# Two attention blocks mixed by a gate: the two products with K of a group in block B stand on either side of the two products for the row maxima

## The chip, the cores and the metric

The kernel runs on one NeuronCore of a Trainium2 chip. The metric is the device time of one execution in microseconds (us). A difference under 0.3% of it cannot be told from none.

## The reference, cut to what matters

Two attention blocks read the same `x` (2048 x 512, 32 heads of 16) and are mixed by a gate for each row. Block A is an attention in four segments of 512 rows with a causal mask inside each, plus a memory `M`, `z` that is carried from segment to segment; block B is a full softmax attention over all 2048 rows.

```python
# A, for each of N = 4 segments
logits = jnp.einsum("bhqd,bhkd->bhqk", qs, ks) * scale + mask
a_dot  = jnp.einsum("bhqk,bhkd->bhqd", _softmax(logits, axis=-1), vs)
o      = g * a_mem + (1.0 - g) * a_dot
...
# B
scores = jnp.einsum("bhqd,bhkd->bhqk", q, k) * (Dh ** -0.5)
o      = jnp.einsum("bhqk,bhkd->bhqd", _softmax(scores, axis=-1), v)
...
return g * a + (1 - g) * b
```

## The kernel before

Up to about 335 us of the profiled execution the kernel projects `x` to Q, K and V and runs A's memory. Then comes the main loop over `k` (L932), 32 **units**. Unit `k` treats four heads of one 512-row chunk of queries, once for block B (`ub = 32 + k`) and once for block A (`ua = k`). It runs over `n`: `n` 0 to 31 are the **groups** of B, 32 to 36 the groups of A. All is written out in program order; each engine works through its own queue in that order and waits at semaphores.

A group of B (`t_group`, L516) treats 128 keys and two of the four heads:

- Two **products with K** (L528), transposed scores, keys on the partitions and 512 queries in the free dimension. The first has its operands on partitions 0 to 63, the second on 64 to 127, so the two stand in two halves of TensorE's rows. Below they are **T0** and **T1**. Each goes to a PSUM bank of its own.
- The banks come from `T3 = TB + [MB]` (`tb0`, `tb1`, `mb`; L848). `bank()` gives out the one that was given out longest ago (L88). So with three banks T0 of a group takes the bank that T1 of the group before the last one had, and T1 takes the bank of T0 of the group just before.
- Two exponentials on ScalarE (L534), **exp0** for T0 and **exp1** for T1, from the bank to the tile `raw8`. A bank is free for the next product when its exponential is done.

Behind the group come the tasks that `plan` holds for `(k, n)`. In B's groups that is, up to unit 30, group 19, one call of `s_b` (L467), in the first groups of unit 0 two: the **products for the maxima** of the *next* unit (128 queries on the partitions, 512 keys in the free dimension), **S1** on rows 64 to 127 first, then **S0** on rows 0 to 63, into the two halves of one of the two buffers `sbk0`, `sbk1`, and one maximum over both on VectorE (L476, **the reduce**). S1 must wait until the reduce of two calls before has left its buffer. `s_a` (L442) does the same for A, in A's groups.

Then `pvs` (L853) issues the **products with V** (L550, all 128 rows) for the tile of keys before, with the exponentials as operand; in the groups `n` = 0 it issues A's last ones and `fin_copy` (L553), a copy of the sums by VectorE. In the group `n` = 1 there are none; from unit 9 on `out_mm` (L612), 12 products of the output projection, stands there.

Other work of VectorE that is queued between the reduces of B's groups: `fin_rec` behind the groups 11 and 13 (L571, two small operations each), `m_chain` behind the group 21 (L480, four), and in every other unit an addition of `out_mm`. Behind the group 24 `m_rows` (L497) issues two products (L501) into a bank of `T3` and a copy on ScalarE.

Of the kernel before, what the change touches and what calls it, by code (L numbers as in the profile page):

```python
# [23 lines left out]
NT = SEQ // 128  # L24
# [10 lines left out]
def gated_mix_kernel(ctx, tc, xt, wq, wk, wv, wo, beta, wqkv, wob, gate_w, out):  # L35
# [52 lines left out]
    def bank(allowed):  # L88
        b = min(allowed, key=lambda a: max([n for n, x in enumerate(lru) if x is a], default=-1))
        lru[:] = [x for x in lru if x is not b] + [b]  # L90
        return b
# [308 lines left out]
    def q_of(u):  # L400
        return QA[u % 2] if u < 32 else QB[u % 3]

    def k_of(u, p):
        return KA[u % 2][:, p] if u < 32 else KB[(u - 32) % 3][:, p]

    def load_q(u):
        kd, qd, c = UN[u]
        load_qk(q_of(u), kd, 0, qd, c)

    def load_ka(u):  # L410
        kd, qd, c = UN[u]
        load_qk(KA[u % 2], kd, 1, qd, c)

    def load_kb(k, c=None):
        dst = KB[k % 3] if c is None else KB[k % 3][:, :, c * C:(c + 1) * C]
        load_qk(dst, "B", 1, k % 8, c)
# [6 lines left out]
    def load_vb(g):  # L423
        v_src(VB[g % 2], "B", g % 4, None)

    def load_va(u):
        kd, qd, c = UN[u]
        v_src(VA[(u // 2) % 2], "A", qd // 2, c)
# [51 lines left out]
    def m_chain(k):  # L480
        mx = pair_max(k)
        if k == 1:
            nc.vector.memset(mx[:, 0], 0.0)
        if k < 32:
            nc.vector.tensor_reduce(mx[:, 1], MXB.pop(32 + k).rearrange("q j p i c -> q (j p) i c"), axis=AX.X,
                                    op=OP.max)
        else:
            nc.vector.memset(mx[:, 1], 0.0)
        del MX[k]
        mx = mx.rearrange("q u h i -> q (u h i)")  # L490
        m8 = M8[k] = W.tile([128, 2, 32], FT, name="m8")
        hi = W.tile([128, 32], FR, name="mhi")
        nc.vector.tensor_scalar(hi, mx, -1.0, None, op0=OP.mult)
        nc.vector.tensor_copy(m8[:, 0], hi)
        nc.vector.scalar_tensor_tensor(m8[:, 1], mx, -1.0, hi, op0=OP.mult, op1=OP.subtract)
# [17 lines left out]

    GA = (((0, (0, 1)),), ((0, (2, 3)),), ((1, (0, 1)), (3, (0, 1))), ((1, (2, 3)), (3, (2, 3))), ((2, (0, 1)), (2, (2, 3))))

    def t_group(u, n, banks):  # L516


        kd, qd, c = UN[u]
        bs = [bank(banks) for _ in range(2)]  # L520
        c0 = 0
        for it, hs in (((n // 2, (n % 2 * 2, n % 2 * 2 + 1)),) if kd == "B" else GA[n]):
            q0 = 128 * it if kd == "A" else 0
            w = C - q0
            pn = it if kd == "B" else it % 2
            for j, h in enumerate(hs):
                r = slice(64 * j, 64 * j + 64)
                nc.tensor.matmul(bs[j][:, c0:c0 + w], k_of(u, h // 2)[r, 128 * it:128 * it + 128],  # L528
                                 q_of(u)[r, h // 2, q0:], start=True, stop=True)
                PT[u, it, h] = PTILE[pn % 2][:, 2 + j if (kd, it) == ("A", 2) else h][:, c0:c0 + w]  # L530
            c0 += w
        for j in range(2):
            pt = PTILE[pn % 2][:, 2 + j if (kd, n) == ("A", 4) else hs[j]]
            nc.scalar.activation(pt, bs[j], AF.Exp, scale=SCALE)  # L534
            if kd == "A":
                m = pt[:, :128] if n < 2 else pt.rearrange("p (a t) -> p a t", a=4)[:, ::3 if n < 4 else 2]
                nc.gpsimd.affine_select(out=m, in_=m, pattern=[[1, 128]] if n < 2 else [[0, 2], [1, 128]],  # L537
                                        compare_op=OP.is_ge, fill=0.0, base=0, channel_multiplier=-1)
# [59 lines left out]
    def load_wo(g):  # L598
        for a, w in enumerate((wo, wob)):
            raw = AT["o"][1][:, g, a]  # L600
            nc.sync.dma_start(raw, w[g * 128:(g + 1) * 128, :])
            nc.gpsimd.tensor_copy(AT["wh"][:, g, a], raw)
            nc.gpsimd.tensor_tensor(AT["wl"][:, g, a], raw, AT["wh"][:, g, a], op=OP.subtract)
# [146 lines left out]
    for blk in range(16):  # L750
# [9 lines left out]
        n = blk + 1 + (c == 2)  # L760
# [74 lines left out]
    def late():  # L835
        proj.close()
        L = AT["L"] = ctx.enter_context(tc.tile_pool(name="late", bufs=1))
        VB[1] = L.tile([128, NT, 8, E + 1], FT, name="vb1")
        AT["o"] = [L.tile([128, 4, 2, C], FT, name=f"o{n}") for n in range(2)]
        AT["wh"] = L.tile([128, 4, 2, DM], FR, name="wh")  # L840
        AT["wl"] = L.tile([128, 4, 2, DM], FR, name="wl")
        AT["d"] = [L.tile([128, C], FT, name=f"d{n}") for n in range(2)]
        AT["oh"] = L.tile([128, 4, 2, 128], FR, name="oh")
        AT["ol"] = L.tile([128, 4, 2, 128], FR, name="ol")
        for p in range(2):
            set_aux(KB[2][:, p], 0)
# [6 lines left out]
    def pvs(k, n):  # L853

        ua, ub = k, 32 + k
        if n == 0:
            if k:
                pv(ua - 1, 2)
                fin_copy(ua - 1)
        elif k == 31 and n < 2 * NT:  # L860
            if n % 2 and n > 1:
                pv(ub, n // 2 - 1)
        elif 2 <= n < 2 * NT + 2:
            pv(ub, n // 2 - 1, n % 2 * 256, n % 2 * 256 + 256)
            if n == 2 * NT + 1:
                fin_copy(ub)
        elif n > 2 * NT + 1:
            m = n - 2 * NT - 2
            if m < 2:
                pv(ua, 0, 256 * m, 256 * m + 256)  # L870
            else:
                pv(ua, 1)
                pv(ua, 3)
# [13 lines left out]
    def beside(k, it):  # L887

        for f, it0, u in ((fin_load, NT + 1, 32 + k), (fin_rec, 5, 31 + k), (fin_bc, 6, 31 + k),
                          (fin_load, 1, k - 1), (fin_rec, 6, k - 1), (fin_bc, S_LAST + 2, k - 1)):  # L890
            if it == it0 and (k or it0 > NT):
                f(u)
        c, j = divmod(k - 1, 8)
        if k and j % 2:
            for kd, it0 in (("B", 9), ("A", 13)):
                if it == it0:
                    fin_norm(kd, j // 2, c)
        if k >= 8 and k % 2 == 0 and it == NT + 2:
            out_split(k // 8 - 1, k // 2 % 4)
        if (k, it) == (31, 4):  # L900
            grest = AT["grest"] = AT["o"][0][64:, 0, 0]
            nc.sync.dma_start(grest, GD[3 * C:].rearrange("(o t) -> o t", o=1).to_broadcast([64, C]))
        if (k, it) == (31, 9):
            grest = AT["grest"]
            nc.vector.tensor_scalar(grest, grest, nh[64:, 3:4], None, op0=OP.mult)
        if (k, it) == (31, NT + 2):
            fin_rec(63)
        if k == 31 and it == 13:
            o = AT["o"][1][:64, 3, 0]
            nc.gpsimd.tensor_tensor(o, o, AT["d"][0][:64], op=OP.mult)  # L910
        if k == 31 and it < 8 and it % 2 == 0:
            for a in range(2):
                tail_split(it // 2, slice(0, 3), a)
# [3 lines left out]
    plan = {}  # L917
# [14 lines left out]
    for k in range(32):  # L932
        ua, ub = k, 32 + k
        banks = T3 + [b[:, 0] for b in SBK] * (k == 31)
        for n in range(NG):
            it = n // 2 if n < NG - 1 else NT + 2
            t_group(*(ub, n) if n < 2 * NT else (ua, n - 2 * NT), banks)
            for f in plan.get((k, n), []) + ex[k][0].get(n, []):
                f()
            pvs(k, n)  # L940
            for f in ex[k][1].get(n, []):
                f()
            if n % 2 == 0 and n < NG - 1:
                continue
            beside(k, it)
            if it == S_LAST:
                m_chain(k + 1)
            if it == 4 and not k:
                late()
            if it == 4 and not k:  # L950
                load_q(ub + 2)
                for c in range(NC4):
                    load_kb(2, c)
            if it == NT and k < 29:
                load_q(ub + 3)
                load_kb(k + 3)
            if it == 6 and k < 31:
                load_q(ua + 1)
                load_ka(ua + 1)
                if (ua + 1) % 2 == 0:  # L960
                    load_va(ua + 1)
            if it == 9:
                if k % 2 == 0 and k < 30:
                    load_vb(k // 2 + 1)
                if 1 <= k <= 4:
                    load_wo(k - 1)
# [55 lines left out]
```

## Time and profile before

| | us |
|---|---|
| median of 3 runs | 1959.55 |
| lowest and highest | 1957.34, 1963.12 |
| profiled execution | 1956.4 |
| its span | 1954.7 |
| busy PE (matmul) in the span | 1930.3 |
| busy DVE (VectorE) | 1629.9 |
| busy ACT (ScalarE) | 1433.4 |
| busy POOL (GpSimd) | 275.8 |

The profile comes from one execution. In a row of the view in order of time stand the start (us from the span's start), the duration (us; of a merged row, from the first start to the last end), the engine, the line of the kernel, the operation, what it writes and reads with buffer numbers left out, and the count; in brackets the idle time ahead of it and what ended that. PE is the matmul itself, PEld the load of its stationary operand. In the trace the reduce is `mxb<-sbk`, an exponential `raw<-tb` or `raw<-mb`, a product with K `tb<-` or `mb<-`, one for the maxima `sbk<-`, one with V `pvb<-`. K of block B lies in `kb` or `xh`, so `tb<-qb,kb` and `tb<-qb,xh` are the same kind of product.

In the view of waits a row has engine, tile, line, what ended the wait, total us, number of waits and the longest.

### The profile page before, as it was taken

How to read it: one execution, taken by the hardware profiler on the slowest of the kernel's cores; microseconds unless marked ns; L12 is line 12 of the kernel's file. 1: busy time of each engine (PE TensorE's matmuls, PEld its weight loads, DVE VectorE, ACT ScalarE, POOL GpSimd, SP SyncE). 2: the span in 40 equal slices, each digit the busy share in tenths (PEclk: the TensorE clock that was granted, in tenths of full speed). 3: DMA queues.
4: the chain of work that ended last, by engine and by line, in shares of the span. 5: the costliest groups of instructions: out<-in, count | busy, mean ns of one | idle time of the engine just before them, and what ended most of it. 6: DMA issues, size and time to landing. Idle time of an engine off the chain costs nothing.

```text
span 1954.7 us, 43539 instructions
## 1 busy us (share of the span) xinstructions
PE 1930.3 (99%) x17485; PEld 939.3 (48%) x17485; DVE 1629.9 (83%) x1798; ACT 1433.4 (73%) x2699; POOL 275.8 (14%) x497
## 2 busy tenths in 40 slices
PE   7999999999999999999999999999999999999999
PEld 5887777444344444444444444444444444444445
DVE  7135766899999999999999999999999999999942
ACT  4233333688888888888888888888888888888884
POOL 5201000012120101111111111111111111111022
PEclk9999999999999999999999999999999999999999
DMA  7666655644444444343435453444354444434111
GB/s 218 170 205 188 198 192 178 156 98 115 98 115 93 106 91 109 81 111 80 114 87 115 87 115 87 113 87 115 87 115 87 109 86 96 101 88 106 48 50 58
DMA packets 163790, 222.49 MB, mean 114 GB/s; under 512 B 39916, under 2 KB 90556, under 8 KB 157828
## 3 DMA queue, kind: packets, MB, share of 16 engines
q1 hardware_dynamic: 159284, 211.41, 43.7%
q0 software_dynamic: 3248, 8.03, 2.1%
q8 instruction: 138, 2.26, 0.5%
q14 instruction: 64, 0.52, 0.1%
q10 hardware_dynamic: 1056, 0.26, 0.1%
HBM read 147.95 MB, written 68.16 MB: 111 GB/s over the span
## 4 chain that ended last, share of the span: by engine, by line
PE 95%; DVE 3%; ACT 1%; SPq 1%; DMA 1%; issue 0%; DVEq 0%; ACTq 0%
PE pvb L550 33%; PE tb L528 17%; PE sbk L474 12%; PE mb L528 9%; PE tb L304 4%; PE sbk L452 3%; PE tb L616 2%; PE mb L304 2%; PE sbk L287 1%; DVE mxb L476 1%; PE tb L287 1%; PE pvb L304 1%; PE mb L616 1%; PE sbk L456 1%; PE mb L287 1%; PE pvb L287 1%
## 5 line engine op out<-in xcount | busy, mean ns | idle before, releaser
L476 DVE TENSOR_REDUCE mxb<-sbk 128x2 f32<-128x1024 f32 x1024 | 1222.3, 1222 | 67.3 <-PE sbk L474 63.1
L534 ACT ACTIVATE raw<-tb 128x512 f32<-128x512 f32 x1555 | 887.5, 598 | 152.9 <-PE tb L528 89.6
L550 PE MATMUL pvb<-raw,vb 128*17 128x256 f32 (+1 forms) x8072 | 639.3, 388 | 0.0
L534 ACT ACTIVATE raw<-mb 128x512 f32<-128x512 f32 x782 | 467.6, 598 | 79.5 <-PE tb L528 44.8
L528 PE MATMUL tb<-qb,xh 64*128 64x512 f32 x872 | 331.6, 495 | 1.7 <-ACT raw L534 1.7
L550 PEld LDWEIGHTS pvb<-raw,vb 128*17 128x17 f32 x8072 | 134.4, 95 | 340.1 <-issue 336.6
L474 PE MATMUL sbk<-xh,qb 64*128 64x512 f32 x1344 | 281.5, 395 | 2.7 <-DVE mxb L476 1.8
L528 PE MATMUL mb<-qb,xh 64*128 64x512 f32 x445 | 220.6, 496 | 0.0
L537 POOL TENSOR_SCALAR_AFFINE_SELECT raw<-raw 128x256 f32<-128x256 f32 (+1 forms) x320 | 115.5, 361 | 709.6 <-ACT raw L534 701.7
L528 PEld LDWEIGHTS tb<-qb,xh 64*128 64x128 f32 x872 | 124.7, 183 | 179.6 <-issue 89.9
L528 PE MATMUL tb<-qb,kb 64*128 64x512 f32 x470 | 179.5, 496 | 1.3 <-DVE st L314 0.8
L460 DVE TENSOR_REDUCE mx<-sbk 128x2 f32<-128x768 f32 (+1 forms) x128 | 136.7, 1090 | 22.9 <-PE sbk L456 18.3
L474 PE MATMUL sbk<-kb,qb 64*128 64x512 f32 x704 | 146.4, 398 | 0.0
L474 PEld LDWEIGHTS sbk<-xh,qb 64*128 64x128 f32 x1344 | 138.3, 186 | 7.4 <-DVE mxb L476 5.0
L528 PEld LDWEIGHTS mb<-qb,xh 64*128 64x128 f32 x445 | 81.3, 183 | 95.2 <-issue 50.4
L590 POOL TENSOR_TENSOR o<-o,d 128x512 f32<-128x512 f32 x31 | 39.7, 1281 | 545.6 <-DMA d<-rd 461.9
L528 PEld LDWEIGHTS tb<-qb,kb 64*128 64x128 f32 x470 | 68.2, 183 | 100.1 <-issue 52.6
L528 PE MATMUL mb<-qb,kb 64*128 64x512 f32 x234 | 116.1, 496 | 0.0
L550 PE MATMUL pvb<-raw,va 128*17 128x256 f32 (+2 forms) x1280 | 94.7, 384 | 0.8 <-ACT pvs L559 0.8
L452 PE MATMUL sbk<-ka,qa 64*128 64x256 f32 (+3 forms) x512 | 88.2, 358 | 1.1
L528 PE MATMUL tb<-qa,ka 64*128 64x512 f32 (+3 forms) x339 | 79.5, 372 | 0.0
L311 ACT ACTIVATE st<-tb 128x512 fp32r<-128x512 f32 x33 | 19.8, 599 | 80.2 <-DVE phi L310 40.5
(284 smaller groups left out, 1837.6 us busy)
## 6 DMA issues: line engine op xcount, KB each, us to landing
xh<-dB SPq DMA_DIRECT2D x38, 512.0 KB
vb<-vdB SPq DMA_DIRECT2D x16, 1088.0 KB
dB<-st SPq DMA_DIRECT2D x64, 256.0 KB
dA<-st SPq DMA_DIRECT2D x64, 256.0 KB
pd<-pvs SPq DMA_DIRECT2D x64, 256.0 KB
kb<-dB SPq DMA_DIRECT2D x22, 512.0 KB
xh<-dB SPq DMA_DIRECT2D x38, 256.0 KB
qb<-dB SPq DMA_DIRECT2D x64, 128.0 KB
```

Source lines behind the costliest of these rows:

```text
L287: nc.tensor.matmul(b, lhs, WV[wi][:, k, :], start=n == 0, stop=n == 11)
L304: nc.tensor.matmul(b, WS[ws][w][wi][:, k, :], (XH, XL)[xi][c][:, k, :], start=n == 0, stop=n == 11)
L452: nc.tensor.matmul(b[:, j, c0:c0 + n], q_of(u)[r, p, i * 128:(i + 1) * 128], k_of(u, p)[r, :n], start=True, stop=False)
L460: nc.vector.tensor_reduce(m[:, :, p, i], b[:, :, :n], axis=AX.X, op=OP.max)
L474: nc.tensor.matmul(b[:, j], q_of(u)[r, p, i * 128:(i + 1) * 128], k_of(u, p)[r, kc * C:(kc + 1) * C], start=True, stop=True)
L476: nc.vector.tensor_reduce(MXB[u][:, :, p, i, kc], b, axis=AX.X, op=OP.max)
L528: nc.tensor.matmul(bs[j][:, c0:c0 + w], k_of(u, h // 2)[r, 128 * it:128 * it + 128], q_of(u)[r, h // 2, q0:], start=True, stop=True)
L534: nc.scalar.activation(pt, bs[j], AF.Exp, scale=SCALE)
L537: nc.gpsimd.affine_select(out=m, in_=m, pattern=[[1, 128]] if n < 2 else [[0, 2], [1, 128]], compare_op=OP.is_ge, fill=0.0, base=0, channe ...
L550: nc.tensor.matmul(PVB[32 * h:32 * h + E + 1, q0 + lo:q0 + hi], vt[:, it, 4 * q + h, :], pt[:, lo:hi], start=it == 0 and lo == 0, stop=it ...
L590: nc.gpsimd.tensor_tensor(o, o, d, op=OP.mult)
L616: nc.tensor.matmul(b, (AT["oh"], AT["ol"])[oi][:, g, a], (AT["wh"], AT["wl"])[wi][:, g, a], start=n == 0, stop=n == 11)
```

## The change

`t_group` takes a list `between` and calls it ahead of the second of the two products. In the main loop the plan's tasks of a group of B are taken out of the plan and given to `t_group` so. The order T0, T1, S1, S0 becomes T0, S1, S0, T1. A's groups and B's groups without a task stay.

```diff
-    def t_group(u, n, banks):
+    def t_group(u, n, banks, between=()):
...
             for j, h in enumerate(hs):
+                if j:
+                    for f in between:
+                        f()
                 r = slice(64 * j, 64 * j + 64)
                 nc.tensor.matmul(bs[j][:, c0:c0 + w], k_of(u, h // 2)[r, 128 * it:128 * it + 128],
                                  q_of(u)[r, h // 2, q0:], start=True, stop=True)
...
-            t_group(*(ub, n) if n < 2 * NT else (ua, n - 2 * NT), banks)
+            mid = plan.pop((k, n)) if n < 2 * NT and (k, n) in plan else []
+            t_group(*(ub, n) if n < 2 * NT else (ua, n - 2 * NT), banks, mid)
             for f in plan.get((k, n), []) + ex[k][0].get(n, []):
                 f()
```

The queue of TensorE, two groups in the middle of unit 9, before (`tb_110`, `tb_111` and `mb` are the three banks, `sbk_115` and `sbk_114` the buffers of the maxima; what a row waits for stands in brackets):

```order
L528 MATMUL tb_111<-qb_70,kb_89 128x512
L528 MATMUL tb_110<-qb_70,kb_89 128x512 [waits Activation_49]
L474 MATMUL sbk_115<-xh_88,qb_69 128x512 [waits DVE_49]
L474 MATMUL sbk_115<-xh_88,qb_69 128x512
L550 MATMUL pvb<-raw_86,vb_75 17x256 x4
L528 MATMUL mb<-qb_70,kb_89 128x512 [waits Activation_49]
L528 MATMUL tb_111<-qb_70,kb_89 128x512 [waits Activation_49]
L474 MATMUL sbk_114<-xh_88,qb_69 128x512 [waits DVE_49]
L474 MATMUL sbk_114<-xh_88,qb_69 128x512
```

And the same groups on the same engine after the change:

```order
L531 MATMUL tb_111<-qb_70,kb_89 128x512
L474 MATMUL sbk_115<-xh_88,qb_69 128x512 [waits DVE_49]
L474 MATMUL sbk_115<-xh_88,qb_69 128x512
L531 MATMUL tb_110<-qb_70,kb_89 128x512 [waits Activation_49]
L553 MATMUL pvb<-raw_86,vb_75 17x256 x4
L531 MATMUL mb<-qb_70,kb_89 128x512 [waits Activation_49]
L474 MATMUL sbk_114<-xh_88,qb_69 128x512 [waits DVE_49]
L474 MATMUL sbk_114<-xh_88,qb_69 128x512
L531 MATMUL tb_111<-qb_70,kb_89 128x512 [waits Activation_49]
```

S1, with its wait for VectorE, has moved ahead of T1, with its wait for ScalarE; nothing else has moved, and each product keeps its bank.

The other place is behind the group 24 of the same unit, on the same engine, where the products of `m_rows` take one of the three banks. Before:

```order
L501 MATMUL mb<-ident,m_7670 32x128 x2
L528 MATMUL tb_111<-qb_70,kb_89 128x512 [waits Activation_49]
L528 MATMUL tb_110<-qb_70,kb_89 128x512 [waits Activation_49]
L474 MATMUL sbk_115<-xh_88,qb_69 128x512 [waits DVE_49]
L474 MATMUL sbk_115<-xh_88,qb_69 128x512
```

After:

```order
L501 MATMUL mb<-ident,m_7670 32x128 x2
L531 MATMUL tb_111<-qb_70,kb_89 128x512 [waits Activation_49]
L474 MATMUL sbk_115<-xh_88,qb_69 128x512 [waits DVE_49]
L474 MATMUL sbk_115<-xh_88,qb_69 128x512
L531 MATMUL tb_110<-qb_70,kb_89 128x512 [waits Activation_49]
```

Here T1 waits for exp1 of the group just before, since `m_rows` took the bank between; that wait now stands behind S1 and S0. The queues of ScalarE, VectorE, GpSimd and of the DMAs are as before.

## Prediction, made blind

> Names used below. A **unit** is one pass of the loop over k: 32 groups of B, then 5 of A. A group issues T0 and T1 (the two products with K; T0 on array rows 0 to 63, T1 on 64 to 127), S1 and S0 (the two products for the maxima, S1 on rows 64 to 127), then the products with V. exp0 and exp1 are ScalarE's exponentials of T0 and T1, the reduce is VectorE's maximum over S0 and S1.
>
> **What bounds the kernel now.** I read first the busy time by stretch, then the chain that ended last.
>
> ```profile
> 400.00:820.00 420.00, 416.68 (x4282) 169.11 (x4280) 401.20 (x414) 357.09 (x667) 56.43 (x105) 1.00 0.45 102
> 820.00:1835.00 1015.00, 1014.28 (x10230) 432.73 (x10230) 939.93 (x960) 838.02 (x1558) 137.85 (x250) 1.00 0.43 98
> ```
>
> ```profile
> PE 95%; DVE 3%; ACT 1%; SPq 1%; DMA 1%; issue 0%; DVEq 0%; ACTq 0%
> ```
>
> The columns of the first view are stretch, length, then busy PE, weight loads, DVE, ACT, POOL. From 820 us PE is busy 99.9%, DVE 92.6% and ACT 82.6%; before 820 us DVE has 95.5%. The clock is 1.00 throughout. The chain is PE for 95% of the span. So PE sets the end, and DVE is close behind it. A busy PE says nothing of waits here, because ends of matmuls are modelled, so I went on to what ended the gaps between weight loads (400 to 1850 us), and to the loads in order of time, since a load carries its product's wait.
>
> The Trainium skill ("Perfetto Trace Analysis", section "Identifying the Most-Contended Engine") says that busy matmul time does not measure how near a kernel is to its limit. Read by busy share alone the change would gain nothing; the starts below agree with the page, since groups of equal work take 1.22 and 1.25 us under the same 99.9%.
>
> ```profile
> PEld tb L528 <- ACT raw L534: 147.7, 350, 0.6
> PEld mb L528 <- ACT raw L534: 72.9, 172, 0.4
> ```
>
> ```profile
> 1042.58 3.69 DVE L476 TENSOR_REDUCE mxb<-sbk 128x2 f32<-128x1024 f32 x3
> 1043.02 0.18 PEld L528 LDWEIGHTS tb<-qb,xh 64*128 64x128 f32 x1 [0.42 <-issue]
> 1043.12 0.19 PEld L474 LDWEIGHTS sbk<-kb,qb 64*128 64x128 f32 x2
> 1043.61 0.60 ACT L534 ACTIVATE raw<-tb 128x512 f32<-128x512 f32 x1 [0.20 <-PE mb L528]
> 1043.68 0.13 PEld L550 LDWEIGHTS pvb<-raw,vb 128*17 128x17 f32 x8 [0.37 <-issue]
> 1044.23 0.21 PEld L528 LDWEIGHTS tb<-qb,xh 64*128 64x128 f32 x2 [0.42 <-ACT raw L534]
> 1044.34 0.21 PEld L474 LDWEIGHTS sbk<-kb,qb 64*128 64x128 f32 x2
> 1044.92 0.13 PEld L550 LDWEIGHTS pvb<-raw,vb 128*17 128x17 f32 x8 [0.37 <-issue]
> 1045.48 0.18 PEld L528 LDWEIGHTS mb<-qb,xh 64*128 64x128 f32 x1 [0.42 <-issue]
> ```
>
> ACT's exponential ended 522 of those gaps; most of each 0.42 us is PE's own, so the starts must give the price. T0 loads at 1043.02; exp0 starts at 1043.61 and ends at 1044.21; its bank goes to T1 of the next group. That pair of loads takes 0.21 us where one takes 0.18: T1 loads at 1044.26, 0.05 after exp0's end and 0.03 after T0. S1 and S0 follow, V waits for both halves, and this group lasts 1.25 us (1044.23 to 1045.48) against 1.21 (1043.02 to 1044.23). Over pairs of groups the difference is 0.022 us: a loop T0, exp0, next T1 that is just longer than PE's own work.
>
> **The change, part by part.**
>
> *T1's wait goes.* T1 moves behind S0, to the second place in its half. How late may a load come there? In unit 0, S1, S0, S1, S0 load in a row:
>
> ```profile
> 335.47 0.42 PEld L474 LDWEIGHTS sbk<-xh,qb 64*128 64x128 f32 x4
> ```
>
> 0.42 less one load of 0.19 leaves 0.23 us from the first to the last: the time one product holds its half. The load in second place starts 0.10 to 0.11 behind T0 (1043.02, 1043.12), while T0's product starts; it is done within 0.11 more, so it may come up to about 0.23 behind T0 unnoticed. The row 1064.78 further on shows it: S1 loads 0.17 behind T0, and V still starts 0.69 behind T0, which is the usual 0.66 (1043.02, 1043.68) and T1's 0.03. So waits of 0.03 us vanish. These are the first (two loads) and the last of such groups in one unit.
>
> ```profile
> 1041.79 0.18 PEld L528 LDWEIGHTS mb<-qb,xh 64*128 64x128 f32 x1 [0.42 <-ACT raw L534]
> 1041.81 0.18 PEld L528 LDWEIGHTS tb<-qb,xh 64*128 64x128 f32 x1
> ...
> 1071.88 0.21 PEld L528 LDWEIGHTS tb<-qb,xh 64*128 64x128 f32 x2 [0.42 <-ACT raw L534]
> ```
>
> There are 12: 12 x 0.022 = 0.26 us a unit. Two longer waits of the same kind, one behind the products of `m_rows` in each unit, one in the second group of every other unit:
>
> ```profile
> 1065.54 0.18 PEld L528 LDWEIGHTS mb<-qb,xh 64*128 64x128 f32 x1 [0.20 <-issue]
> 1065.76 0.18 PEld L528 LDWEIGHTS tb<-qb,xh 64*128 64x128 f32 x1
> 1065.77 0.29 PEld L474 LDWEIGHTS sbk<-xh,qb 64*128 64x128 f32 x2
> ```
>
> ```profile
> 1083.36 0.18 PEld L528 LDWEIGHTS tb<-qb,kb 64*128 64x128 f32 x1 [0.42 <-issue]
> 1083.54 0.18 PEld L528 LDWEIGHTS mb<-qb,kb 64*128 64x128 f32 x1
> ```
>
> They are 0.22 and 0.18, both under 0.23, so both vanish. Gain: 0.26 + 0.22 + 0.18/2 = 0.57 us a unit.
>
> *S1's wait comes forward.* S1 stood behind T1 in its half: its load too could come 0.23 after T0 at no cost. Now it stands at T0, and each hundredth that its bank comes later than T0 is paid; S0 and T1 are queued behind it, V behind T1. Behind V stands the next T0. In a plain group it waits for nothing: the first reduce above ends at 1042.58 + 1.22 = 1043.80, with the handover 1043.85, and the bank is wanted at 1044.23, 0.38 later. Where VectorE has other work it is late:
>
> ```profile
> L476 DVE TENSOR_REDUCE mxb<-sbk 128x2 f32<-128x1024 f32 x1024 | 1222.3, 1222 | 67.3 <-PE sbk L474 63.1
> ```
>
> ```profile
> 1052.91 3.48 DVE L476 TENSOR_REDUCE mxb<-sbk 128x2 f32<-128x1024 f32 x3
> 1054.08 0.18 PEld L528 LDWEIGHTS tb<-qb,xh 64*128 64x128 f32 x1 [0.42 <-ACT raw L534]
> 1054.19 0.21 PEld L474 LDWEIGHTS sbk<-kb,qb 64*128 64x128 f32 x2
> ```
>
> ```profile
> 1062.99 4.77 DVE L476 TENSOR_REDUCE mxb<-sbk 128x2 f32<-128x1024 f32 x4
> 1064.09 0.18 PEld L528 LDWEIGHTS mb<-qb,xh 64*128 64x128 f32 x1 [0.42 <-ACT raw L534]
> 1064.26 0.19 PEld L474 LDWEIGHTS sbk<-xh,qb 64*128 64x128 f32 x2
> 1064.78 0.13 PEld L550 LDWEIGHTS pvb<-raw,vb 128*17 128x17 f32 x8 [0.33 <-issue]
> ```
>
> Behind the two `fin_rec` the first of three reduces ends at 1054.13, so S1 cannot load before 1054.19; T0 is at 1054.08 and, with two T1 waits gone since that queue formed, at 1054.04. Hold: 0.15. Behind `m_chain` the bank comes at 1064.26 and T0 is at 1064.09 less 0.02: hold 0.19. Reduces in a row are (3.48 - 1.22)/2 = 1.13 apart, a group 1.22, so each hold also relieves the groups behind it. Loss 0.34 us a unit.
>
> *Units 9 to 29* (with output products): 0.57 - 0.34 = 0.23 us, x 21 = 4.8 us. *Units 1 to 8* have no output products, and their third group follows without products with V:
>
> ```profile
> 639.34 0.18 PEld L528 LDWEIGHTS tb<-qb,kb 64*128 64x128 f32 x1 [0.15 <-ACT raw L534]
> 639.46 0.39 PE L528 MATMUL tb<-qb,kb 64*128 64x512 f32 x1
> 640.13 0.18 PEld L528 LDWEIGHTS tb<-qb,kb 64*128 64x128 f32 x1 [0.61 <-ACT raw L534]
> 640.18 5.74 DVE L476 TENSOR_REDUCE mxb<-sbk 128x2 f32<-128x1024 f32 x5
> 641.35 0.18 PEld L528 LDWEIGHTS mb<-qb,kb 64*128 64x128 f32 x1 [0.42 <-issue]
> 641.46 0.19 PEld L474 LDWEIGHTS sbk<-xh,qb 64*128 64x128 f32 x2
> ```
>
> T1 comes 0.79 late there and S behind it; with S ahead, one slot of 0.23 is saved. But the reduce that starts at 640.18 frees its bank at 641.45, and the next T0 would come at 641.35 - 0.23 = 641.12: S1 is held 0.33. So gain 0.23 + 0.26 + 0.22 = 0.71, loss 0.33 + 0.15 + 0.19 = 0.67: 0.04 x 8 = 0.3 us. Units 0 and 30, where gains and holds are fewer, I take as nothing.
>
> *The new pairing.* T0 beside S1 and S0 beside T1 start nowhere together in this trace. At 1065.77 S0 loads beside a late T1 and V follows in the usual time. A product T that stands last could be thought slower (L528 takes 0.50 against 0.39 of L474), but the one at 639.46, behind another, takes 0.39: the 0.11 is its load. From both sides I bound the cost by the rows' last digit, 0.01 us a group, x 980 groups = 10 us either way, and take nothing.
>
> *What is late next.* exp1 must wait for T1, 0.23 later; but it started 0.49 after exp0 anyway, so ACT covers that. exp0, the order on ACT, DVE, SP and POOL, the DMAs and all other waits stay. No DMA moves.
>
> The sum is 4.8 + 0.3 = 5.1 us. The profiled execution took 1956.4 us (span 1954.7), so 1951.3; it was 3.15 below the median of the runs, 1959.55, which gives **1954.5**.
>
> **Rivals.** *All of the gain is kept*: S1's waits cost nothing, since T1 has room behind them. Then 0.57 x 21 = 12 us, 1947.5. Against it: at 1065.76 T1 waits, and S0, whose half is free, loads only at 1065.77: what stands behind a waiting load is held in both halves. The Trainium skill ("TensorE: Matmul & The Clock Gate", section "The mechanism") says that matmuls keep strict program order. That row agrees; by the page this rival falls.
>
> *DVE becomes the bound (slower)*: S1's wait costs a full slot of 0.23 at four groups a unit (behind the copy of the sums, behind `fin_rec`, behind `m_chain`, and once more in a run), 0.92 x 29 = 26.7 us, against gains of 0.57 x 21 + 0.71 x 8 = 17.7: +9, 1968.5. It decides where the holds of a unit pass 17.7/29 = 0.61 us. For it speak the runs of late reduces and DVE's 92.6 to 95.5%; against it the 1.13 between reduces.
>
> *T1's lateness never cost anything*, or the holds eat exactly the gain: 1959.5. For it stands PE's 99.9%; against it the 1.21 and 1.25 above.
>
> **How the numbers follow.** Forecast 0.52 (own range 1950 to 1959), gain kept 0.13, DVE the bound 0.20, nothing 0.15. Differences under 0.3% (5.9 us; below 1953.7 is faster) cannot be told from none in this kernel. Of the forecast's 0.52 about 0.25 lies beyond that, since every other unit gains 0.32 and waits of 0.02 in single groups are not all counted. Faster 0.25 + 0.13 = 0.38, same 0.27 + 0.15 = 0.42, slower 0.20. The range 1946 to 1966 holds the forecast with the pairing's 10 us on either side; it leaves out some of the rival at 1947.5 and over half of that at 1968.5, about 0.16.
>
> **What would show it.** Right: plain groups of 1.22 us without every second 1.24; loads of T1 0.11 behind T0, with S1 beside T0; S1 0.15 to 0.2 behind T0 only after `fin_rec` and `m_chain`, and 0.3 in the fourth group of units 1 to 8. Wrong: S1 late in most groups, plain groups longer than 1.22, or V later than 0.67 after T0.

## The result and the profile after

| | before | changed |
|---|---|---|
| median of 5 runs, us | 1958.53 | 1949.88 |
| lowest and highest, us | 1957.34, 1963.12 | 1947.33, 1951.2 |
| ratio, with its 95% interval | 1 | 0.9955 (0.9944 to 0.9965) |
| profiled execution, us | 1956.4 | 1949.85 |
| its span, us | 1954.7 | 1948.1 |

The kernel became 8.65 us faster, where 5.1 had been forecast. The main loop, taken in the two traces from its first product with K to its last `fin_copy`, became 10.61 us shorter. The profiled execution shows only 6.55 of it, because its front, the code ahead of that product, which the change doesn't touch, took 4.05 us longer than in the profiled execution of before. The unequal clock of that stretch stands in the last section.

The first two views for the changed kernel, busy time by stretch and the shares of the chain, tell as little as before. PE is busy 99.9% of both stretches (before 99.2% and 99.9%), it has 95% of the chain again, and the same work is done in less time:

```profile
400.00:820.00 420.00, 419.47 (x4330) 169.81 (x4327) 401.84 (x415) 359.11 (x670) 58.66 (x110) 1.00 0.47 104
820.00:1835.00 1015.00, 1014.28 (x10296) 427.76 (x10296) 946.12 (x967) 844.62 (x1569) 138.59 (x250) 1.00 0.44 98
```

In the view of waits ACT's exponential still ends 524 gaps between loads, 218.7 us in all (before 522, 220.6). That sum hardly moves, since these gaps are mostly PE's own time; read as a price, it would have said that nothing changed.

```profile
PEld tb L531 <- ACT raw L537: 145.8, 352, 0.4
PEld mb L531 <- ACT raw L537: 72.9, 172, 0.4
```

The loads in order of time show what did change. These are the changed kernel's ordinary groups 14 and 15 of unit 14, then group 16, behind the two `fin_rec` (S1 and S0 share one row, which lasts from S1's start to S0's end; rows left out are marked):

```profile
1052.17 0.18 PEld L531 LDWEIGHTS tb<-qb,xh 64*128 64x128 f32 x1 [0.42 <-ACT raw L537]
1052.17 0.29 PEld L474 LDWEIGHTS sbk<-kb,qb 64*128 64x128 f32 x2
1052.28 0.19 PEld L531 LDWEIGHTS tb<-qb,xh 64*128 64x128 f32 x1
1052.83 0.13 PEld L553 LDWEIGHTS pvb<-raw,vb 128*17 128x17 f32 x8 [0.37 <-issue]
1053.39 0.18 PEld L531 LDWEIGHTS mb<-qb,xh 64*128 64x128 f32 x1 [0.42 <-issue]
...
1054.61 0.18 PEld L531 LDWEIGHTS tb<-qb,xh 64*128 64x128 f32 x1 [0.42 <-ACT raw L537]
1054.75 0.19 PEld L474 LDWEIGHTS sbk<-kb,qb 64*128 64x128 f32 x2
1054.86 0.19 PEld L531 LDWEIGHTS mb<-qb,xh 64*128 64x128 f32 x1
...
1055.97 0.18 PEld L531 LDWEIGHTS tb<-qb,xh 64*128 64x128 f32 x1 [0.42 <-issue]
```

In group 14 S1 loads beside T0, S0 and T1 0.11 later, V 0.66 behind T0, and the group lasts 1.22 us (1052.17 to 1053.39); of the 525 ordinary groups in units 9 to 29 one lasts over 1.235 us, where 160 did before. In group 16 S1 is late: it loads 0.14 behind T0, everything behind it moves by as much, and the group lasts 1.36 (1054.61 to 1055.97). Behind `m_chain`, in group 24, it is 0.17, and the next group, behind the products of `m_rows` (L501), has no wait for T1 any more:

```profile
1064.51 0.18 PEld L531 LDWEIGHTS mb<-qb,xh 64*128 64x128 f32 x1 [0.42 <-ACT raw L537]
1064.68 0.19 PEld L474 LDWEIGHTS sbk<-xh,qb 64*128 64x128 f32 x2
...
1065.58 0.33 PEld L501 LDWEIGHTS tb<-ident,m 128*32 128x32 f32 x4
1066.11 0.18 PEld L531 LDWEIGHTS mb<-qb,xh 64*128 64x128 f32 x1 [0.20 <-issue]
1066.11 0.29 PEld L474 LDWEIGHTS sbk<-xh,qb 64*128 64x128 f32 x2
```

The reduce itself keeps its length, and VectorE's idle time ahead of it falls from 67.3 to 57.7 us, since groups are shorter:

```profile
L476 DVE TENSOR_REDUCE mxb<-sbk 128x2 f32<-128x1024 f32 x1024 | 1222.0, 1222 | 57.7 <-PE sbk L474 25.4
```

All this stands in the forecast. What doesn't is group 20. First before, then the changed kernel, each from T0 of group 20 to T0 of group 21:

```profile
1058.99 0.21 PEld L528 LDWEIGHTS tb<-qb,xh 64*128 64x128 f32 x2 [0.42 <-ACT raw L534]
1059.20 0.41 PEld L474 LDWEIGHTS sbk<-xh,qb 64*128 64x128 f32 x2
...
1060.41 0.18 PEld L528 LDWEIGHTS mb<-qb,xh 64*128 64x128 f32 x1 [0.42 <-issue]
```

```profile
1059.62 0.18 PEld L531 LDWEIGHTS tb<-qb,xh 64*128 64x128 f32 x1 [0.42 <-ACT raw L537]
1059.63 0.29 PEld L474 LDWEIGHTS sbk<-xh,qb 64*128 64x128 f32 x2
1059.74 0.19 PEld L531 LDWEIGHTS tb<-qb,xh 64*128 64x128 f32 x1
...
1060.85 0.18 PEld L531 LDWEIGHTS mb<-qb,xh 64*128 64x128 f32 x1 [0.42 <-issue]
```

It lasted 1.42 us and now lasts 1.22 (1.23 by the rounded starts). It is the first group whose S reads Q and K of the next unit (in these rows `xh`, in the groups ahead of it `kb`). Ahead of its S loads stand four waits for DMAs, each an instruction of its own on PE's queue, as the view of line 474 on that queue shows, before and after:

```profile
L474 PEldq EVENT_SEMAPHORE  x4: 51/51/51, 1059.0 to 1059.4; - x4
```

```profile
L474 PEldq EVENT_SEMAPHORE  x4: 51/51/51, 1058.9 to 1059.4; - x4
```

The two rows look alike; what they stand beside does not. The single records of the traces, starts in us:

```
          T0's load  T1's load  waits ahead of S1    S1's load  waits ahead of S0    S0's load
before     1058.988   1059.014  1059.010, 1059.121   1059.197   1059.247, 1059.353   1059.428
changed    1059.625   1059.737  1058.852, 1058.963   1059.629   1059.271, 1059.377   1059.734
```

In the changed kernel all four start at least 0.25 us ahead of T0's load, two of them even ahead of the loads of V's products of the group before (1059.07). In the kernel before they run only from the moment at which T1's bank came free, behind T1 in the program, and S0 loads 0.44 behind T0, 0.21 past the 0.23 of room that the prediction found. That is the 0.20 us by which the group was longer.

### The profile page after: what moved, and what is told of

Its sections match the earlier page's. It is cut to its first block, busy times and chain, and to the rows that moved or that the text cites. A ratio compares the mean times of both kernels' runs of the same rounds, so it can differ in the third digit from the quotient of the medians.

```text
span 1948.1 us, 43539 instructions
## 1 busy us (share of the span) xinstructions
PE 1926.0 (99%) x17485; PEld 931.7 (48%) x17485; DVE 1628.4 (84%) x1798; ACT 1436.2 (74%) x2699; POOL 277.0 (14%) x497
## 4 chain that ended last, share of the span: by engine, by line
PE 95%; DVE 2%; DMA 2%; SPq 0%; ACT 0%; issue 0%; DVEq 0%; ACTq 0%
PE pvb L553 33%; PE tb L531 17%; PE sbk L474 12%; PE mb L531 9%; PE tb L304 5%; PE sbk L452 3%; PE tb L619 2%; PE mb L304 2%; PE sbk L287 1%; PE tb L287 1%; PE pvb L304 1%; PE mb L619 1%; DMA pd<-pvs 1%; PE sbk L456 1%; PE mb L287 1%; PE pvb L287 1%
## 5 line engine op out<-in xcount | busy, mean ns | idle before, releaser
L476 DVE TENSOR_REDUCE mxb<-sbk 128x2 f32<-128x1024 f32 x1024 | 1222.0, 1222 | 57.7 <-PE sbk L474 25.4
L474 PE MATMUL sbk<-xh,qb 64*128 64x512 f32 x1344 | 475.2, 445 | 2.9 <-DMA xh<-dB 2.0
L531 PE MATMUL tb<-qb,xh 64*128 64x512 f32 x872 | 353.2, 443 | 0.0
L474 PE MATMUL sbk<-kb,qb 64*128 64x512 f32 x704 | 239.4, 444 | 0.2 <-DVE mxb L476 0.2
L531 PEld LDWEIGHTS tb<-qb,xh 64*128 64x128 f32 x872 | 146.4, 185 | 176.6 <-issue 89.7
L531 PE MATMUL mb<-qb,xh 64*128 64x512 f32 x445 | 198.8, 447 | 0.0
L474 PEld LDWEIGHTS sbk<-xh,qb 64*128 64x128 f32 x1344 | 189.1, 185 | 8.0 <-DVE mxb L476 4.3
L531 PE MATMUL tb<-qb,kb 64*128 64x512 f32 x470 | 191.9, 446 | 0.8 <-DVE st L314 0.8
L531 PEld LDWEIGHTS tb<-qb,kb 64*128 64x128 f32 x470 | 79.2, 184 | 98.9 <-issue 53.1
L531 PE MATMUL mb<-qb,kb 64*128 64x512 f32 x234 | 104.0, 445 | 0.0
L474 PEld LDWEIGHTS sbk<-kb,qb 64*128 64x128 f32 x704 | 95.2, 184 | 5.7 <-issue 3.2
```

What stands on the lines that cost most here:

```text
L474: nc.tensor.matmul(b[:, j], q_of(u)[r, p, i * 128:(i + 1) * 128], k_of(u, p)[r, kc * C:(kc + 1) * C], start=True, stop=True)
L476: nc.vector.tensor_reduce(MXB[u][:, :, p, i, kc], b, axis=AX.X, op=OP.max)
```

## The theory behind the experiments

The theory has four parts. A T1 whose bank is late costs its lateness, and nothing in second place, up to 0.23 us. An S1 whose reduce is late now costs its lateness too. A T1 that waits keeps PE's queue from executing the semaphore waits that stand behind it, which costs 0.20 us in group 20. The two halves of the array take their loads side by side. Rivals: the whole gain is the ordinary groups' and `m_rows`'s, group 20's waits being idle by-standers; or the holds of S1 are paid back by the groups behind them.

A unit's change is measured in the profiled executions from one `fin_copy` to the next and compared with the same unit of before. Units 9 to 29 are summed (21 units), since all of them have the same code but for the addition of every other unit.

| kernel | new order in | units 9 to 29, us | a unit, us | ratio to before, 95% |
|---|---|---|---|---|
| changed | all groups with S | -9.59 | -0.46 | 0.9955 (0.9944 to 0.9965) |
| e1 | group 20 | -4.15 | -0.20 | 0.9959 (0.9946 to 0.9971) |
| e2 | all but group 20 | -5.35 | -0.25 | 0.9974 (0.9965 to 0.9983) |
| e3 | all but the holds and unit 0 | -15.31 | -0.73 | 0.9889 (0.9874 to 0.9904) |
| e4 | all, S0 ahead of S1 | -7.73 | -0.37 | 0.9967 (0.9954 to 0.9979) |
| e5 | group 25 | -4.88 | -0.23 | 0.9966 (0.9954 to 0.9979) |
| e6 | ordinary groups | -4.23 | -0.20 | 0.9967 (0.9956 to 0.9977) |
| e7 | group 20, as T0, S1, T1, S0 | -4.61 | -0.22 | 0.9975 (0.9966 to 0.9984) |

The medians beside which e1 to e4 stand are 1960.01 us for the kernel before, those of e5 to e7 1958.59. A ratio of medians also holds the front and unit 0, and scatters: e1's median fell by 8.78 us and its loop by 5.17. So sizes are read from the units.

## The experiments

**e1, group 20 alone.** Every other group in the old order (each diff is against the changed kernel):

```diff
-            mid = plan.pop((k, n)) if n < 2 * NT and (k, n) in plan else []
+            mid = plan.pop((k, n)) if n < 2 * NT and (k, n) in plan and n == 20 else []
```

> The old order everywhere but in the group 20 of each unit, the first that uses the Q and K of the unit after the next, where S1 and S0 wait for the DMAs. Theory (T1's wait kept PE's queue from taking the four semaphore waits of these products ahead of time): that group falls from 1.425 to 1.22 us, 0.2 x 30 = 6 us, ratio 0.997, about 1952.5; the four waits stand ahead of T0's load. Rival (only T1's own 0.02 goes): 0.02 x 30 = 0.6 us, ratio 0.9997.

Measured: 1951.23 us, 0.9959 (0.9946 to 0.9971). The loop became 5.17 us shorter, half of the changed kernel's 10.61, by one group of a unit's 32. Its rows:

```profile
1056.38 0.18 PEld L531 LDWEIGHTS tb<-qb,xh 64*128 64x128 f32 x1 [0.42 <-ACT raw L537]
1056.38 0.29 PEld L474 LDWEIGHTS sbk<-xh,qb 64*128 64x128 f32 x2
1056.49 0.19 PEld L531 LDWEIGHTS tb<-qb,xh 64*128 64x128 f32 x1
...
1057.59 0.18 PEld L531 LDWEIGHTS mb<-qb,xh 64*128 64x128 f32 x1 [0.42 <-issue]
```

1.21 us between the two T0. The rival falls.

**e2, all but group 20.** The same line with `n != 20`.

> The new order everywhere but in the group 20. Theory: 0.2 x 30 = 6 us of the gain are lost, ratio 0.9985 (0.998 to 0.9995), and the forecast's own sum of 5 us less unit 0's loss is what is left. Rival (the group has no part in it): 0.9955, as the changed kernel.

Measured: 1955.1 us, 0.9974 (0.9965 to 0.9983). That is a little more gain than the theory's number and much less than the rival's. By units it fits: 0.25 us a unit against 0.46 with group 20, the difference of 4.24 us over 21 units being 0.20 in each. Its unit 0 was 2.35 us longer than before. The changed kernel's is 0.84 longer; the rest lies in group 2, which lasts 6.88 us instead of the changed kernel's 5.33, and there the granted clock (the third number from the end; 1.00 in the changed kernel) fell:

```profile
345.00:350.00 5.00, 4.88 (x15) 3.60 (x15) 2.33 (x3) 0.71 (x2) 0.28 (x1) 0.66 0.69 230
```

**e3, the old order where S1 is held.** That is behind the two `fin_rec` and `m_chain`, in the groups 3 to 5 of units 1 to 8, and in unit 0:

```diff
-            mid = plan.pop((k, n)) if n < 2 * NT and (k, n) in plan else []
+            late_bank = (16, 17, 24) + (3, 4, 5) * (k < 9)
+            mid = plan.pop((k, n)) if k and n < 2 * NT and n not in late_bank and (k, n) in plan else []
```

> The new order, but the old one in the groups where S1's bank comes late (16, 17 and 24, and 3 to 5 in units 1 to 8) and in all of unit 0. Theory (the holds of S1 are paid by PE one for one): 0.12 + 0.155 = 0.275 x 29 = 8 us, 0.2 x 8 = 1.6 us and 0.85 us in unit 0 come back beyond the changed kernel: ratio 0.990 to 0.9915, about 1940. Rival (VectorE sets the pace there, so that a hold saved in one group is paid in the next): ratio 0.9945 to 0.996, as the changed kernel.

Measured: 1938.44 us (1934.65 to 1940.12), 0.9889 (0.9874 to 0.9904), faster than both kernels. Group 16 in it:

```profile
1046.07 0.18 PEld L531 LDWEIGHTS tb<-qb,xh 64*128 64x128 f32 x1 [0.42 <-ACT raw L537]
1046.09 0.18 PEld L531 LDWEIGHTS mb<-qb,xh 64*128 64x128 f32 x1
1046.23 0.19 PEld L474 LDWEIGHTS sbk<-kb,qb 64*128 64x128 f32 x2
1046.75 0.13 PEld L553 LDWEIGHTS pvb<-raw,vb 128*17 128x17 f32 x8 [0.34 <-issue]
1047.31 0.19 PEld L531 LDWEIGHTS tb<-qb,xh 64*128 64x128 f32 x2 [0.42 <-issue]
```

S1 is as late as in the changed kernel, 0.16 behind T0, but it stands second in its half: V follows 0.68 behind T0 and the group lasts 1.24. Over units 9 to 29 this is 5.72 us better than the changed kernel, 0.27 a unit. In the mean of these units the groups 16 and 24 last 1.36 and 1.60 us in the changed kernel and 1.24 and 1.45 here; the groups behind them, 17 and 25, differ by 0.003 at most. So the holds are paid one for one, and the groups behind them pay nothing back. The whole loop is 10.31 us shorter than the changed kernel's, where 10.4 had been expected.

**e4, S0 ahead of S1.** The changed kernel, and in `s_b` the other order, so that the program reads T0, S0, S1, T1:

```diff
-        for j in (1, 0):
+        for j in (0, 1):
```

> The changed kernel with S0 ahead of S1, so T0, S0 in one half of the rows and then S1, T1 in the other. Theory (each half takes its own loads, and only a wait at a semaphore holds what stands behind it in both): S1 still starts beside T0, same time as the changed kernel, ratio 0.995 to 0.9965. Rival (products start strictly in program order): S1 starts 0.11 us behind T0 and T1 as much later, 0.1 x 980 = 98 us longer, ratio 1.045.

Measured: 1953.8 us, 0.9967 (0.9954 to 0.9979). An ordinary group looks as in the changed kernel:

```profile
1053.60 0.18 PEld L531 LDWEIGHTS mb<-qb,xh 64*128 64x128 f32 x1 [0.42 <-issue]
1053.60 0.29 PEld L474 LDWEIGHTS sbk<-kb,qb 64*128 64x128 f32 x2
1053.71 0.19 PEld L531 LDWEIGHTS tb<-qb,xh 64*128 64x128 f32 x1
```

By the single records the first S load, at 1053.602, is S1's, though S0 stands ahead of it in the program: S0, which carries the wait for VectorE, loads at 1053.704, 0.11 behind T0, as every load in second place does. The products start in the same order, S1's at 1053.604 and S0's at 1053.932. The halves take their loads side by side, and S1 comes 0.006 behind T0 where the changed kernel has 0.003. Where S0's wait is real, in group 16, it loads 0.146 behind T0 and S1, behind it, at 0.150: there it does hold up the other half. This kernel is 0.09 us a unit behind the changed one, 32 x 0.003; the two medians cannot be told apart.

**e5, group 25 alone** (the one behind `m_rows`): the line of e1 with `n == 25`.

> New order in group 25 alone (behind the products of m_rows); all other groups as before. Theory (a late T1 costs what its bank comes late, and second place hides it whole): group 25 goes from 1.434 us to 1.225, 0.21 us in each of some 30 units, -6.3 us, ratio 0.9968 (0.996 to 0.9975), groups 16, 20 and 24 unchanged. Rival (a late T1 cost little by itself, the gain of the changed kernel being that of group 20): the next groups take back what group 25 gains, ratio 0.999 or more.

Measured: 1951.28 us, 0.9966 (0.9954 to 0.9979); group 25 of unit 14 goes from 1.434 to 1.215:

```profile
1066.71 0.18 PEld L531 LDWEIGHTS mb<-qb,xh 64*128 64x128 f32 x1 [0.20 <-issue]
1066.71 0.29 PEld L474 LDWEIGHTS sbk<-xh,qb 64*128 64x128 f32 x2
1066.94 0.18 PEld L531 LDWEIGHTS tb<-qb,xh 64*128 64x128 f32 x1
1067.37 0.13 PEld L553 LDWEIGHTS pvb<-raw,vb 128*17 128x17 f32 x8 [0.25 <-issue]
```

T1 is as late as before, 0.23 behind T0, and V follows 0.66 behind T0 all the same. The room of a load in second place is thus at least 0.23 us.

**e6, the ordinary groups alone** (one line replaced by two):

```diff
-            mid = plan.pop((k, n)) if n < 2 * NT and (k, n) in plan else []
+            apart = (1, 16, 17, 20, 24, 25) + (3, 4, 5) * (k < 9)
+            mid = plan.pop((k, n)) if k and n < 2 * NT and n not in apart and (k, n) in plan else []
```

> New order in the ordinary groups alone: old order in all of unit 0, in groups 1, 16, 17, 20, 24 and 25, and in 3 to 5 of units 1 to 8. Theory (the 0.022 us of every second group is real): about 11 groups of 0.022, 0.24 us a unit from unit 9 on and 0.2 before, -7 us, ratio 0.9965 (0.9955 to 0.9975), ordinary groups of 1.22 us throughout and group 20 at 1.42. Rival (0.022 us is exp0's loop, which comes back elsewhere, in the groups left in the old order or in those of A): ratio 0.999 to 1.000. The gains of this run, of group 25 alone and of group 20 alone should add up to nearly that of the run with the old order at the holds: -7 - 6.3 - 5.2 with 0.18 more for group 1 of every other unit, -20 against the -21 us of the loop seen there.

Measured: 1951.5 us, 0.9967 (0.9956 to 0.9977). 0.20 us a unit, where 0.24 had been expected from 11 groups. The ordinary groups last 1.22, but only nine of them had the wait before (6 to 14, 18, 22, 28 and 30 of the even ones), and 9 x 0.022 is 0.20. The sum nearly holds in units 9 to 29: 0.20 (e1) + 0.23 (e5) + 0.20 (e6) = 0.63, with 0.08 for the second group 0.71, and e3 has 0.73. This run's unit 0, all in the old order, was 1.52 us longer than before; 1.46 of it is group 20, where S waited for a DMA (waits from 380 to 384 us):

```profile
PE sbk L474 <- DMA xh<-dB: 1.2, 1, 1.2
```

**e7, a dose between.** In group 20 alone, T1 between S1 and S0; the other groups as before:

```diff
         for j in (1, 0):
+            if not j and HALF:
+                HALF.pop()()
...
+            mid = plan.pop((k, n)) if n == 20 and (k, n) in plan else []
```

`HALF` holds the call that issues T1, put there by `t_group`.

> In group 20 alone the order T0, S1, T1, S0; all other groups as before. The waits for the next unit's Q and K are two of S1's and two of S0's. Theory (only waits behind a held T1 run late, and S0, second in its half, has 0.23 us of room): S1's two run ahead, S0's two put its load about 0.21 us behind T0, V comes 0.67 behind T0 as usual, group 20 takes 1.22 to 1.24 us, -0.2 us a unit, -5.5 us, ratio 0.997 (0.996 to 0.998). Rival (each of the four waits that runs behind T1 costs its 0.05 us): group 20 takes about 1.32, -0.1 us a unit, -3 us, ratio 0.9985. Second rival (the four waits have nothing to do with it, the order of S1, S0 and T1 has): group 20 stays at 1.42, ratio 1.000.

Measured: 1953.75 us, 0.9975 (0.9966 to 0.9984). The interval nearly reaches the first rival's 0.9985; the trace decides. In this kernel the products with K are L532, those for the maxima L477, V is L560:

```profile
1060.75 0.18 PEld L532 LDWEIGHTS tb<-qb,xh 64*128 64x128 f32 x1 [0.42 <-ACT raw L544]
1060.75 0.18 PEld L477 LDWEIGHTS sbk<-xh,qb 64*128 64x128 f32 x1
1060.86 0.19 PEld L532 LDWEIGHTS tb<-qb,xh 64*128 64x128 f32 x1
1060.95 0.18 PEld L477 LDWEIGHTS sbk<-xh,qb 64*128 64x128 f32 x1
1061.41 0.13 PEld L560 LDWEIGHTS pvb<-raw,vb 128*17 128x17 f32 x8 [0.28 <-issue]
1061.97 0.18 PEld L532 LDWEIGHTS mb<-qb,xh 64*128 64x128 f32 x1 [0.42 <-issue]
```

By the single records S1's two waits run at 1059.966 and 1060.077, far ahead; S0's two, now behind T1, run at 1060.770 and 1060.876, after T0's load at 1060.747. Half of the waits are late again, S0 loads 0.20 behind T0 instead of 0.44, and that is within the 0.23 of room: the group lasts 1.22. So a wait that runs late costs nothing by itself, but only what it carries past that room.

## Why the prediction was right, and the step that it lacked

**The direction and the mechanism were right; the size lacked a term.** In us a unit, for units 9 to 29:

| term of the sum | forecast | measured | by |
|---|---|---|---|
| T1's waits of 0.03 in ordinary groups | 0.26 | 0.20 | e6 |
| group 25, behind `m_rows` | 0.22 | 0.23 | e5 |
| second group of every other unit | 0.09 | 0.08 | starts of T0 in the changed kernel |
| holds of S1 in groups 16 and 24 | -0.34 | -0.27 | e3 against the changed kernel |
| group 20 | not named, 0 | 0.20 | e1, e7 |
| sum | 0.23 | 0.44 | changed kernel: 0.46 |

The 0.02 that is left lies in A's groups.

*T1's wait goes.* Its three terms hold. The 0.20 is less than 0.26 because nine ordinary groups had the wait; the twelve counted hold the groups 16 and 24 too, and one too many. The second group lasts 3.61 us instead of 3.78 in the units with the long wait, and 0.02 longer than before in the others. The row shows T1 still 0.18 behind T0 there, with S in between and the output products 0.67 behind T0, where they stood 0.84 behind:

```profile
1083.66 0.18 PEld L531 LDWEIGHTS tb<-qb,kb 64*128 64x128 f32 x1 [0.42 <-issue]
1083.66 0.29 PEld L474 LDWEIGHTS sbk<-xh,qb 64*128 64x128 f32 x2
1083.84 0.18 PEld L531 LDWEIGHTS mb<-qb,kb 64*128 64x128 f32 x1
1084.33 0.77 PEld L619 LDWEIGHTS tb<-wh,oh 128*128 128x128 f32 x4 [0.31 <-ACT raw L537]
```

*S1's wait comes forward.* In units 9 to 29 the places are those named, and no others. The holds were forecast at 0.15 and 0.19 and are 0.147 and 0.179 by the single records of unit 14. The price of 0.27 is smaller than their sum, because in e3 the same two groups still pay T1's 0.02 each, which the forecast had counted among the twelve.

*Units 1 to 8.* Forecast 0.04 a unit. Units 2, 4, 5 and 7 gain 0.20 to 0.29: the same 0.20 for group 20 is missing. The total of 1.89 us, 0.24 a unit, fits by luck. In the profile of before an operation of `m_chain` in unit 3 (L495) took 1.28 us instead of 0.18 and made group 24 there 1.0 longer; in the changed kernel's units 1, 6 and 8 group 16 held S1 for 0.31, 0.57 and 0.68. The hold of the fourth group was put at 0.33 against a slot of 0.23; it is 0.29, and the third group, though S1 comes 0.38 behind T0 there, gains 0.19 or 0.20 (2.01 us before, 1.82 now). The changed kernel's fourth group:

```profile
596.71 0.18 PEld L531 LDWEIGHTS mb<-qb,xh 64*128 64x128 f32 x1 [0.42 <-issue]
597.00 0.19 PEld L474 LDWEIGHTS sbk<-kb,qb 64*128 64x128 f32 x2
```

*Unit 0 was taken as nothing.* The whole unit is 0.84 longer in this profile; with its code unchanged it was equal in e3. In the groups 2, 4 and 6, with two calls of `s_b`, a loss can be read: T1 now stands behind the second S1, which waits for a reduce just begun. They last 5.33, 5.04 and 5.05 us, before 5.09, 4.79 and 4.87. Group 8, with one call, goes from 1.59 to 1.82: its S1 waits 0.6 for its bank, and T1 behind it.

*The new pairing* was bounded at 10 us either way and taken as nothing. Ordinary groups of 1.219 us in the mean, in the changed kernel as in e6, where those without a wait had 1.217 to 1.221 before, put it below 0.005 us a group.

**The step that failed** is in what the prediction says is late next: every wait that stood *behind* T1 was looked at for its bank alone. "the DMAs and all other waits stay" is true of the waits' number and not of when they can be executed. Group 20 in the trace of before had S0 0.44 behind T0 and lasted 1.42 us; it was in plain sight, and it was not asked why. With 0.20 x 30 = 6 us for it and 0.9 less for unit 0's four groups the working would have given 10.2 us, against the 10.61 of the loop; that they are so near is luck in part, by the single waits of units 1 to 8.

**The rivals.** *DVE becomes the bound* needed holds of 0.61 us a unit; they are 0.33. *All of the gain is kept* gave 1947.5, and the measured 1949.88 lies nearer to it than to the forecast, but not by its mechanism: e3 shows that the holds are paid. Its sum also left out units 1 to 8; with the 0.71 x 8 that the other rival counts it is 1941.9. *Nothing* falls by the interval.

The sentence used against *All of the gain is kept* was too broad. The Trainium skill ("TensorE: Matmul & The Clock Gate", section "The mechanism") has matmuls in strict program order; the row at 1065.77 agreed because T1 was waiting there. In e4 S1 loads 0.10 ahead of an S0 that stands ahead of it, and its product starts 0.33 ahead of S0's, so here the order holds across the halves only for what stands behind a waiting load. The rival fell by the holds, which need no more than that.

## What to carry to other kernels

A product that waits for a semaphore holds up the semaphore waits behind it as well, so put products whose buffer may be late behind those that read new data for the first time, and look for groups that last longer than their neighbours with the same work. Where two waits can each stand in the place that has no room, the order should change from group to group with whichever is late: e3 did that, from unit 9 on at three groups a unit, and gained 21 us where one order for all gained 9. A gain found in a wait should be looked for in every group by itself before it is multiplied.

## What the runs showed of the hardware

- **PE's queue runs ahead of its loads.** Semaphore waits that are instructions of their own (0.051 us each, 0.11 apart) were executed up to 0.77 us ahead of T0's load, during earlier products, unless a load ahead of them was itself waiting (changed kernel against before; e7 has two on either side in one group).
- **A load in second place in its half has at least 0.23 us of room**: T1 at 0.23 in e5 and S0 at 0.20 in e7 cost nothing; S0 at 0.44 cost 0.20.
- **The front's time differs between executions of one code**, and its clock with it. In the eight other profiled executions the front took from 0.6 us less to 5.4 us more than in before's. From 320 to 340 us the granted clock (the third number from the end) was full in the profile of before and 0.91 in that of the changed kernel:

```profile
320.00:340.00 20.00, 19.43 (x92) 13.87 (x92) 12.31 (x18) 6.14 (x15) 2.74 (x5) 1.00 0.64 196
```

```profile
320.00:340.00 20.00, 19.04 (x90) 14.02 (x90) 12.11 (x17) 4.26 (x11) 2.75 (x5) 0.91 0.66 193
```

The clock is not all of it: e3's front had before's clock in this stretch (1.00) and from 40 to 80 us (0.96) and took 1.3 us longer. What sets the clock was not tried. A difference of single profiles must leave the front out, and look at the clock in unit 0 too (e2).
